# Transposing q and k in quarters, four at a time, in a fused attention and token-mixing kernel

## The chip, the cores and the metric

The kernel runs on one core of one Trainium2 chip. The metric is device time in microseconds for one execution of the whole program, the median over runs.

## The reference

For each of 4 batches and 8 heads of 64 channels, attention over 768 tokens in which a query sees the 96 tokens up to itself and the first 8 tokens; then a mixing block on the result.

```python
scores = (q @ k.T) / sqrt(D) - slope[h] * dist          # kept: local window of 96, and 8 global keys
a = softmax(where(keep, scores, -1e9));  x = a @ v      # x as [B, 768, 512]
theta = x @ w_theta
y = w_tok_r @ (x * cos(theta)) + w_tok_i @ (x * sin(theta))
u = x + y;  out = u + relu(u @ w_ch)
```

## The kernel before

Work is cut in tiles of 128 tokens, six to a batch, and heads go in pairs: the two heads of a pair fill the 128 partitions with their 64 channels each. A query tile needs the keys of its own tile and of one more tile (the previous one, whose first 8 columns are replaced by the global keys), so the scores of a pair are 11 blocks of 128x128 in three groups (`GROUPS`): group 0 holds tiles 0 and 1, groups 1 and 2 two tiles each.

Every instruction is put on its engine in the order in which the program is written (`K` keeps program order), so the order below is set by hand. For each pair of heads:

- `att_transpose` brings q and k of the pair from token-major to channel-major. It issues 12 TensorE transposes for q and 12 for k (six token tiles, two heads), each with a 128x64 block of q or k as the stationary operand and a 128x128 identity as the moving one, into two PSUM tiles `ps_tr` of one bank each, one for q and one for k. Then ScalarE copies k and VectorE or ScalarE (`q_eng`) copies q to SBUF (`kT`, `qT`). The copy interleaves: token number 6p+t of a head lies at partition p, place t, so the copies read with a stride.
- `att_extras`, on GpSimd, makes the key tiles in which the first 8 columns are the global keys (`kT[:, S:]`, lines 233 and 234), and `prepare_v` does the same for v (lines 91 and 92). The loads of the next batch (`load_heads`) stand behind them in GpSimd's queue.
- `att_scores` computes one group's scores in a two-bank PSUM tile `ps_w` (two buffers); the two heads of the pair use the two row halves of the array. ScalarE exponentiates it (line 279), VectorE multiplies by the mask and bias factors (`att_mul`, lines 290 and 292).
- `att_values` multiplies by v, with 65 columns of which the last sums the weights, and VectorE normalises.

Batch 0's attention runs first by itself with a different path for the bias. The attention of batches 1 to 3 runs inside `attend_beside`, between the token mixing (`mix_tok`, line 403, 128x512 matmuls) of the batch before. For each pair the order is: scores of group 0, four or eight mixing matmuls, scores of groups 1 and 2, the transposes of the next pair, eight mixing matmuls (`m(2)`), the values of this pair. The transposes for the first pair of a batch stand outside this loop: for batch 1 among the set-up of the token weights, for batches 2 and 3 between the theta matmuls of the batch before (`mix_theta`, line 368), whose sines ScalarE computes with another table (lines 376 and 377). `turn_u` sends u through a DMA transpose on SyncE's queue, and `mix_ch` (line 445) waits for it.

Of the kernel before, what the change touches and what calls it, by code (L numbers as in the profile page):

```python
# [10 lines left out]
BF = mybir.dt.bfloat16  # L11
# [5 lines left out]
def kernel(  # L17
# [13 lines left out]
    nc = tc.nc  # L31
    B, H, S, D = q.shape
    T = 128
    NT = S // T
    DM = H * D
    NC = DM // T
    NG = int(n_global)
# [11 lines left out]
    abuf = ctx.enter_context(tc.tile_pool(name="abuf", bufs=3))  # L49
# [4 lines left out]
    K = tc.keep_in_program_order  # L54

    def ps_wide():
        return psum.tile([T, 2, DM], FP, name="ps_w", tag="ps_w", bufs=2)
# [4 lines left out]
    def ps_tr(cols):  # L62
        return psum.tile([T, cols], BF, name="ps_tr", tag="ps_tr", bufs=2)
# [4 lines left out]
    q_sb, k_sb, x_sb = {}, {}, {}  # L68
# [19 lines left out]
    def prepare_v(b, h0, eng=nc.gpsimd):  # L88
        hs = slice(h0, h0 + 2)
        vs, vp = v_sb[b % 2], v_pv[b % 2]  # L90
        K(eng.tensor_copy(out=vp[:, hs, :, :], in_=vs[:, hs, 1:NT - 1, :]))
        K(eng.tensor_copy(
            out=vp[0:NG, hs, :, :],
            in_=vs[0:NG, hs, 0:1, :].to_broadcast([NG, 2, NT - 2, D + 1])))
# [56 lines left out]
    ident = const.tile([T, T], BF)  # L151
# [50 lines left out]
    for g_, blocks in enumerate(GROUPS):  # L202
        for i_, key in enumerate(blocks):
            where[key] = (g_, i_)
    qTs, kTs, exps, probs, values = {}, {}, {}, {}, {}
    xTs, zris, css = {}, {}, {}

    def att_transpose(b, h0, extras=True, sins=None, q_eng="dve", between=None, cuts=(T,)):
        pq, pk = ps_tr(S), ps_tr(S)
        for src, pst in ((q_sb[b], pq), (k_sb[b], pk)):  # L210
            if pst is pk and between is not None:
                between()
            for t_ in range(NT):
                for hh in range(2):
                    K(nc.tensor.transpose(pst[hh * D:(hh + 1) * D, t_ * T:(t_ + 1) * T],  # L215
                                          src[:, h0 + hh, t_ * D:(t_ + 1) * D], ident))
        if sins is not None:
            sins()

        kT = abuf.tile([T, S + (NT - 2) * T], BF, name="kT", bufs=2)  # L220
        qT = abuf.tile([T, S], BF, name="qT", bufs=2)
        copy = nc.scalar.copy if q_eng == "act" else nc.vector.tensor_copy
        for op, dst, src in ((nc.scalar.copy, kT[:, 0:S], pk), (copy, qT, pq)):
            for p0, p1 in zip((0,) + cuts, cuts):
                K(op(out=dst.rearrange("a (p t) -> a p t", t=NT)[:, p0:p1, :],  # L225
                     in_=src.rearrange("a (t p) -> a p t", t=NT)[:, p0:p1, :]))
        qTs[b, h0], kTs[b, h0] = qT, kT
        if extras:
            att_extras(b, h0)

    def att_extras(b, h0, eng=nc.gpsimd, values=True):
        kT = kTs[b, h0]
        K(eng.tensor_copy(out=kT[:, S:], in_=kT[:, T:S - T]))  # L233
        K(eng.tensor_copy(
            out=kT[:, S:].rearrange("a (t p) -> a t p", p=T)[:, :, 0:NG],
            in_=kT[:, None, 0:NG].to_broadcast([T, NT - 2, NG])))
        if eng is nc.gpsimd and values:
            prepare_v(b, h0)
# [3 lines left out]
    def att_bias(h0, g_):  # L242

        ps = biased[h0, g_] = ps_wide()
        rows = dist.rearrange("a n t -> a (n t)")
        for hh in range(2):
            if g_ == 0:
                out_, rhs = ps[:, hh, 0:3 * T], rows
            else:
                out_ = ps[:, hh, :].rearrange("a (r x) -> a r x", r=2)  # L250
                rhs = rows[:, None, T:3 * T].to_broadcast([T, 2, 2 * T])
            K(nc.tensor.matmul(out_, lhsT=ident_d[:, h0 + hh, :], rhs=rhs,
                               start=True, stop=False))

    def att_scores(b, h0, g_, mul=True):
        qT, kT = qTs[b, h0], kTs[b, h0]
        blocks = GROUPS[g_]
        n = len(blocks)
        bias = b == 0 and g_ != 1
        if bias and (h0, g_) not in biased:  # L260
            att_bias(h0, g_)
        ps = biased[h0, g_] if bias else ps_wide()

        runs = [(0, 2)] + [(2, 1)] if g_ == 0 else [(i_, 1) for i_ in range(n)]
        for i_, w in runs:
            it, prev = blocks[i_]
            kc = it * T if prev == 0 else (0 if it == 1 else S + (it - 2) * T)
            for hh in range(2):
                R = slice(D * hh, D * (hh + 1))
                K(nc.tensor.matmul(ps[:, hh, i_ * T:(i_ + w) * T],  # L270
                                   lhsT=kT[R, kc:kc + T], rhs=qT[R, it * T:(it + w) * T],
                                   start=not bias, stop=not bias or i_ == n - 1))
        if bias:
            p = abuf.tile([T, 2, 4 * T], BF, name="p", bufs=6)
            K(nc.scalar.activation(p[:, :, 0:n * T], ps[:, :, 0:n * T], AF.Exp, scale=scale))
            probs[b, h0, g_] = p
            return
        e = abuf.tile([T, 2, 4 * T], BF, name="e", bufs=3)
        K(nc.scalar.activation(e[:, :, 0:n * T], ps[:, :, 0:n * T], AF.Exp, scale=scale))  # L279
        exps[b, h0, g_] = e  # L280
        if mul:
            att_mul(b, h0, g_)

    def att_mul(b, h0, g_):
        e = exps[b, h0, g_]
        n = len(GROUPS[g_])
        p = abuf.tile([T, 2, 4 * T], BF, name="p", bufs=6)
        hs = slice(h0, h0 + 2)
        if g_ == 0:
            K(nc.vector.tensor_mul(p[:, :, 0:n * T], e[:, :, 0:n * T], wmask[:, hs, :]))  # L290
        else:
            K(nc.vector.tensor_mul(  # L292
                p.rearrange("a h (r x) -> a h r x", r=2),
                e.rearrange("a h (r x) -> a h r x", r=2),
                wmask[:, hs, None, T:3 * T].to_broadcast([T, 2, 2, 2 * T])))
        probs[b, h0, g_] = p
# [179 lines left out]
    def attend_beside(b, main, lead, load):  # L476


        def m(n=1):
            for _ in range(n):  # L480
                main.pop(0)()

        m(lead)
        for h0 in range(0, H, 2):
            att_scores(b, h0, 0)
            m(2 if h0 else 1)
            att_scores(b, h0, 1)
            att_scores(b, h0, 2)
            if h0 + 2 < H:
                att_transpose(b, h0 + 2, q_eng="act")  # L490
                if load and h0 == 0:
                    load_heads(b + 1, 0, 4)
                if load and h0 + 4 == H:
                    load_heads(b + 1, 4, 4)
                m(2)
            else:
                if load:
                    turn_x(b, NC - 2, False)
                m(len(main) - 1)
            att_values(b, h0)  # L500
            if h0 + 2 < H and not (load and h0 + 4 == H):
                turn_x(b, h0 // 2, True)
        m()
# [4 lines left out]
    for src, dst in ((first[:, 0], q_sb[0]), (first[:, 1], k_sb[0])):  # L508
        K(nc.vector.tensor_copy(out=dst[:, 0:2, :], in_=src))
    att_bias(0, 0)  # L510
    att_transpose(0, 0, extras=False, between=lambda: keep_warm(1), cuts=(43, T))
    make_ident_d(2, 6)
    att_extras(0, 0, nc.vector)
    prepare_v(0, 0, nc.vector)
    keep_warm(1)
    att_scores(0, 0, 0)
    att_scores(0, 0, 1)
    att_transpose(0, 2, extras=False)
    att_extras(0, 2, nc.gpsimd, False)
    prepare_v(0, 2)  # L520
    load_wtok(0)
# [118 lines left out]
```

## Time and profile before

| | |
|---|---|
| median of 3 runs | 174.29 us (173.44 to 175.55) |
| profiled execution | 173.54 us, span 171.8 us |
| granted TensorE clock | 1.0 |
| busy: PE / weight load / VectorE / ScalarE / GpSimd | 94% / 51% / 67% / 60% / 35% of the span |
| transposes of q and k (line 215) | 384 matmuls, 16.5 us busy |
| copies of them out of PSUM (line 225), ScalarE and VectorE | 12.9 + 7.5 us and 6.8 us busy |

Matmuls are pipelined, so the busy time of one (219 ns for a transpose) is its latency, not what it costs in a row of others; the distance between starts gives that. A wait is put down to what released the engine.

### The profile page before, as it was taken

Reading aid. Unit: us, or ns where it says so; the run is one execution under the profiler, and the core shown is the slowest. Engines: PE = TensorE matmul, PEld = TensorE weight load, DVE = VectorE, ACT = ScalarE, POOL = GpSimd, SP = SyncE. Lnnn points to the kernel's source line nnn. Section 1 sums busy time; section 2 is a strip of 40 time slices with the busy share of each in tenths; the row PEclk is TensorE's granted clock in tenths of the full one; section 3 lists DMA queues with packets and bytes.
Section 4 is the critical chain, followed back from the end, with each engine's and each line's share of the span. In section 5 each row is a group of like instructions: output and inputs, shape, how many; then the busy total and the mean of one; then the engine's idle time right before and its main releaser. Section 6 shows DMA issues by size and latency. Waiting matters only on the chain.

```text
span 171.8 us, 4076 instructions
## 1 busy us (share of the span) xinstructions
PE 162.1 (94%) x1700; PEld 87.5 (51%) x1700; DVE 114.2 (67%) x210; ACT 103.0 (60%) x120; POOL 60.9 (35%) x99
## 2 busy tenths in 40 slices
PE   7669999999999999999999998999999999999992
PEld 2246665556465654536556553545655544444441
DVE  7878865965858774767587694748567766634362
ACT  5969887947676562798658604798756708400010
POOL 8996797004672820033944700044134000000000
PEclk9999999999999999999999999999999999999999
DMA  5999999999999999910699999911433642233325
GB/s 151 188 170 189 209 211 209 196 183 179 173 142 148 114 229 199 250 64 4 81 167 118 152 210 197 213 65 22 89 77 94 84 152 86 96 34 61 103 109 185
DMA packets 57058, 24.05 MB, mean 140 GB/s; under 512 B 43088, under 2 KB 54096, under 8 KB 57040
## 3 DMA queue, kind: packets, MB, share of 16 engines
q0 software_dynamic: 35328, 12.45, 69.2%
q1 hardware_dynamic: 21440, 10.95, 29.6%
q10 hardware_dynamic: 272, 0.39, 0.7%
q8 instruction: 13, 0.21, 0.6%
q14 instruction: 5, 0.04, 0.1%
HBM read 25.69 MB, written 6.29 MB: 186 GB/s over the span
## 4 chain that ended last, share of the span: by engine, by line
PE 76%; DMA 9%; DVE 6%; POOL 3%; ACT 2%; issue 2%; DVEq 0%; POOLq 0%; ACTq 0%
PE ps_mm L403 34%; PE ps_mm L445 11%; PE ps_w L368 10%; PE ps_w L270 6%; PE ps_tr L215 6%; DMA uTd<-u 5%; PE ps_w L319 4%; DMA v_sb<-in_v_dram 4%; DVE w_tokT L117 2%; PE ps_mm L319 2%; PE ps_tr L114 1%; DVE zri L384 1%; ACT e L279 1%; DVE p L292 1%; ACT kT L225 1%
## 5 line engine op out<-in xcount | busy, mean ns | idle before, releaser
L403 PE MATMUL ps_mm<-zri,w_tokT 128*128 128x512 bf16 x288 | 68.7, 380 | 0.1
L279 ACT ACTIVATE e<-ps_w 128x1024 bf16<-128x1024 f32 (+1 forms) x40 | 37.1, 958 | 18.4 <-PE ps_w L270 18.4
L403 PEld LDWEIGHTS <-w_tokT 128*128 128x128 bf16 x288 | 26.2, 98 | 30.7 <-issue 2.3
L233 POOL COPY kT<-kT 128x512 bf16<-128x512 bf16 x15 | 9.6, 643 | 68.8 <-ACT kT L225 68.7
L292 DVE TENSOR_TENSOR p<-e,wmask 128x1024 bf16<-128x1024 bf16 x28 | 19.9, 709 | 12.2 <-ACT e L279 12.2
L376 ACT ACTIVATE cs<-ps_w,halfpi 128x1024 bf16<-128x1024 f32 x12 | 13.4, 1116 | 19.9 <-PE ps_w L368 19.8
L408 DVE TENSOR_TENSOR u<-x_sb,ps_mm 128x512 bf16<-128x512 bf16 x24 | 16.2, 683 | 12.5 <-PE ps_mm L403 12.5
L368 PE MATMUL ps_w<-w_theta_bf,xT 128*128 128x512 bf16 x96 | 22.8, 379 | 0.3 <-ACT cs L377 0.3
L445 PE MATMUL ps_mm<-w_ch_bf,uTd 128*128 128x512 bf16 x88 | 22.5, 379 | 0.5 <-DMA uTd<-u 0.5
L384 DVE TENSOR_TENSOR zri<-cs,x_sb 128x1024 bf16<-128x1024 bf16 x24 | 16.1, 690 | 9.7 <-ACT cs L376 8.4
L270 PE MATMUL ps_w<-qT,kT 64*128 64x128 bf16 (+1 forms) x320 | 16.0, 223 | 2.8 <-DVE qT L225 1.3
L448 DVE SCALAR_TENSOR_TENSOR o_sb<-ps_mm,u 128x512 f32<-128x512 f32 (+2 forms) x25 | 16.5, 665 | 1.1 <-PE ps_mm L445 0.9
L270 PEld LDWEIGHTS <-kT 64*128 64x128 bf16 x320 | 9.3, 94 | 12.8 <-issue 8.5
L225 ACT COPY kT<-ps_tr 128x768 bf16<-128x768 bf16 (+2 forms) x17 | 12.9, 765 | 2.9 <-PE ps_tr L215 2.8
L319 PEld LDWEIGHTS <-p 128*128 128x128 bf16 x352 | 12.7, 97 | 3.7 <-DVE p L292 0.5
L368 PEld LDWEIGHTS <-xT 128*128 128x128 bf16 x96 | 8.9, 98 | 10.9 <-issue 0.5
L445 PEld LDWEIGHTS <-uTd 128*128 128x128 bf16 x88 | 8.1, 97 | 9.9 <-DMA uTd<-u 1.2
L80 POOL DMA_DIRECT2D v_sb<-in_v_dram x10 | 13.1, 1309 | 0.0
L377 ACT ACTIVATE cs<-ps_w 128x1024 bf16<-128x1024 f32 x12 | 12.2, 1020 | 0.0
L327 DVE TENSOR_TENSOR x_sb<-ps_w,rec 128x768 bf16<-128x768 f32 x12 | 11.5, 958 | 0.4
L319 PE MATMUL ps_w<-v_sb,p 128*128 128x65 bf16 x168 | 10.3, 193 | 0.0
L430 ACT COPY uT<-ps_tr 128x512 bf16<-128x512 bf16 x1 | 0.6, 586 | 15.5 <-PE ps_tr L426 15.5
(79 smaller groups left out, 189.5 us busy)
## 6 DMA issues: line engine op xcount, KB each, us to landing
out_dram<-o_sb SPq DMA_DIRECT2D x23, 256.0 KB, 3.0
q_sb<-in_q_dram POOLq DMA_DIRECT2D x6, 384.0 KB, 7.7
k_sb<-in_k_dram POOLq DMA_DIRECT2D x6, 384.0 KB, 10.4
v_sb<-in_v_dram POOLq DMA_DIRECT2D x6, 384.0 KB, 15.1
w_nat<-in_moe_w_tok_r_dram POOLq DMA_DIRECT2D x1, 1152.0 KB, 12.5
w_nat<-in_moe_w_tok_i_dram POOLq DMA_DIRECT2D x1, 1152.0 KB, 13.6
v_sb<-in_v_dram POOLq DMA_DIRECT2D x4, 192.0 KB, 7.2
q_sb<-in_q_dram POOLq DMA_DIRECT2D x3, 192.0 KB, 6.7
```

The costliest lines, as they stand in the source:

```text
L225: K(op(out=dst.rearrange("a (p t) -> a p t", t=NT)[:, p0:p1, :], in_=src.rearrange("a (t p) -> a p t", t=NT)[:, p0:p1, :]))
L270: K(nc.tensor.matmul(ps[:, hh, i_ * T:(i_ + w) * T], lhsT=kT[R, kc:kc + T], rhs=qT[R, it * T:(it + w) * T], start=not bias, stop=not bias ...
L279: K(nc.scalar.activation(e[:, :, 0:n * T], ps[:, :, 0:n * T], AF.Exp, scale=scale))
L292: K(nc.vector.tensor_mul(p.rearrange("a h (r x) -> a h r x", r=2), e.rearrange("a h (r x) -> a h r x", r=2), wmask[:, hs, None, T:3 * T].t ...
L319: K(nc.tensor.matmul(dst, lhsT=lhsT, rhs=rhs, start=(i_ == 0), stop=(i_ == len(mms) - 1)))
L368: K(nc.tensor.matmul(pth[:, s2, :], lhsT=xTs[b][:, dc, c:c + T], rhs=w_theta_bf[:, dc, :], start=(dc == 0), stop=(dc == NC - 1)))
L376: K(nc.scalar.activation(cs[:, :, 0, :], pth, AF.Sin, bias=halfpi))
L384: K(nc.vector.tensor_mul(zris[b][:, st:st + 2, wi, :].rearrange("a s (c d) -> a s c d", d=T), cs[:, :, wi, :].rearrange("a s (c d) -> a s ...
L403: K(nc.tensor.matmul(acc, lhsT=w_tokT[wi][:, st, tt * T:(tt + 1) * T], rhs=zris[b][:, st, wi, :], start=(done[b, tt] == 0), stop=(done[b, ...
L408: K(nc.vector.tensor_add(us[b][:, tt, :].rearrange("a (c d) -> a c d", d=T), x_sb[b][:, :, tt, :], acc.rearrange("a (c d) -> a c d", d=T)))
L445: K(nc.tensor.matmul(pc[:, 0:N], lhsT=uT[:, c:c + T], rhs=w_ch_bf[:, dc, cols], start=(dc == 0), stop=(dc == NC - 1)))
L448: K(nc.vector.scalar_tensor_tensor(o_sb, in0=pc[:, 0:N], scalar=0.0, in1=us[b][:, tt, cols], op0=ALU.max, op1=ALU.add))
```

## The change

For batches 1 to 3, a 128x64 block is no longer transposed whole. Its 128 tokens are halved, so that each transpose takes 64 tokens by 64 channels: the row half of the array follows the token half `r`, the column half follows the head `hh`. Four such quarters, two heads by two token halves, follow one another in the queue, first of k and then of q for each tile. The two row halves write to two different PSUM banks, so a bank now holds q and k of one token half (`halves[r]`), where it held all tokens of q or of k. There are still two copies to SBUF: ScalarE takes the first bank, and the engine that copied q takes the second; each writes its half of q and of k into one combined tile `qk`. The copy of keys with the global columns, `mT`, is now a part of that tile. Batch 0 keeps whole transposes, but uses the combined tile.

```diff
     def att_transpose(b, h0, extras=True, sins=None, q_eng="dve", between=None, cuts=(T,)):
+        qk = abuf.tile([T, 2 * S + (NT - 2) * T], BF, name="qk", bufs=2)
+        kT, qT = qk[:, 0:S], qk[:, S:2 * S]
+        qTs[b, h0], kTs[b, h0] = qT, kT
+        mTs[b, h0] = qk[:, 2 * S:]
+        copy = nc.scalar.copy if q_eng == "act" else nc.vector.tensor_copy
+        if b > 0:
+            HP = T // 2
+            halves = [ps_tr(S), ps_tr(S)]
+            for t_ in range(NT):
+                for i_, src in enumerate((k_sb[b], q_sb[b])):
+                    c = (i_ * NT + t_) * HP
+                    for r in range(2):
+                        P = slice(r * HP, (r + 1) * HP)
+                        for hh in range(2):
+                            K(nc.tensor.transpose(
+                                halves[r][hh * D:(hh + 1) * D, c:c + HP],
+                                src[P, h0 + hh, t_ * D:(t_ + 1) * D], ident[P, P]))
+            if sins is not None:
+                sins()
+            for r, op in enumerate((nc.scalar.copy, copy)):
+                K(op(out=qk[:, 0:2 * S].rearrange("a (i r p t) -> a i r p t",
+                                                  i=2, r=2, t=NT)[:, :, r, :, :],
+                     in_=halves[r].rearrange("a (i t p) -> a i p t", i=2, t=NT)))
+            if extras:
+                att_extras(b, h0)
+            return
         pq, pk = ps_tr(S), ps_tr(S)
...
-        kT = abuf.tile([T, S + (NT - 2) * T], BF, name="kT", bufs=2)
-        qT = abuf.tile([T, S], BF, name="qT", bufs=2)
...
     def att_extras(b, h0, eng=nc.gpsimd, values=True):
-        K(eng.tensor_copy(out=kT[:, S:], in_=kT[:, T:S - T]))
+        K(eng.tensor_copy(out=mT, in_=kT[:, T:S - T]))
...
     def att_scores(b, h0, g_, mul=True):
-            kc = it * T if prev == 0 else (0 if it == 1 else S + (it - 2) * T)
+            if prev == 0 or it == 1:
+                keys = kT[:, (it - prev) * T:(it - prev + 1) * T]
+            else:
+                keys = mT[:, (it - 2) * T:(it - 1) * T]
```

More of the change, by code (lines that the diff above doesn't have):

```diff
@@ L204 @@
             where[key] = (g_, i_)
-    qTs, kTs, exps, probs, values = {}, {}, {}, {}, {}
+    qTs, kTs, mTs = {}, {}, {}
+    exps, probs, values = {}, {}, {}
     xTs, zris, css = {}, {}, {}
     def att_transpose(b, h0, extras=True, sins=None, q_eng="dve", between=None, cuts=(T,)):
+        qk = abuf.tile([T, 2 * S + (NT - 2) * T], BF, name="qk", bufs=2)
[24 more added lines that the diff above has]
+            return
         pq, pk = ps_tr(S), ps_tr(S)
@@ L216, in att_transpose @@
                                           src[:, h0 + hh, t_ * D:(t_ + 1) * D], ident))
-        if sins is not None:
-            sins()
-        kT = abuf.tile([T, S + (NT - 2) * T], BF, name="kT", bufs=2)
-        qT = abuf.tile([T, S], BF, name="qT", bufs=2)
-        copy = nc.scalar.copy if q_eng == "act" else nc.vector.tensor_copy
-        for op, dst, src in ((nc.scalar.copy, kT[:, 0:S], pk), (copy, qT, pq)):
+        for op, dst, src in ((nc.scalar.copy, kT, pk), (copy, qT, pq)):
             for p0, p1 in zip((0,) + cuts, cuts):
@@ L226, in att_transpose @@
                      in_=src.rearrange("a (t p) -> a p t", t=NT)[:, p0:p1, :]))
-        qTs[b, h0], kTs[b, h0] = qT, kT
         if extras:
@@ L232, in att_extras @@
         kT = kTs[b, h0]
-        K(eng.tensor_copy(out=kT[:, S:], in_=kT[:, T:S - T]))
+        mT = mTs[b, h0]
+        K(eng.tensor_copy(out=mT, in_=kT[:, T:S - T]))
         K(eng.tensor_copy(
-            out=kT[:, S:].rearrange("a (t p) -> a t p", p=T)[:, :, 0:NG],
+            out=mT.rearrange("a (t p) -> a t p", p=T)[:, :, 0:NG],
             in_=kT[:, None, 0:NG].to_broadcast([T, NT - 2, NG])))
@@ L255, in att_scores @@
     def att_scores(b, h0, g_, mul=True):
-        qT, kT = qTs[b, h0], kTs[b, h0]
+        qT, kT, mT = qTs[b, h0], kTs[b, h0], mTs[b, h0]
         blocks = GROUPS[g_]
@@ L270, in att_scores @@
                 K(nc.tensor.matmul(ps[:, hh, i_ * T:(i_ + w) * T],
-                                   lhsT=kT[R, kc:kc + T], rhs=qT[R, it * T:(it + w) * T],
+                                   lhsT=keys[R, :], rhs=qT[R, it * T:(it + w) * T],
                                    start=not bias, stop=not bias or i_ == n - 1))
```

## Prediction

> **What bounds the kernel now.** I read the page first (busy shares and the chain that ended last), then the groups by shape, then the timeline of one repetition of the changed step.
>
> ```profile
> span 171.8 us, 4076 instructions
> PE 162.1 (94%) x1700; PEld 87.5 (51%) x1700; DVE 114.2 (67%) x210; ACT 103.0 (60%) x120; POOL 60.9 (35%) x99
> ...
> PE 76%; DMA 9%; DVE 6%; POOL 3%; ACT 2%; issue 2%; DVEq 0%; POOLq 0%; ACTq 0%
> ```
>
> PE is busy 94% of the span and holds 76% of the chain. Read alone, that says that a microsecond taken from the transposes is a microsecond gained. The stage says otherwise. Here is one head pair of a later batch (batch 1, the transposes of pair 4) from the timeline; columns are start, length, engine, line, tiles and count:
>
> ```profile
> 47.22 0.62 PE L270 MATMUL ps_w<-qT,kT 64*128 64x128 bf16 x16
> 47.66 1.94 ACT L279 ACTIVATE e<-ps_w 128x1024 bf16<-128x1024 f32 x2 [1.36 <-PE ps_w L270]
> 47.77 0.53 PE L215 MATMUL ps_tr<-ident,q_sb 128*64 128x128 bf16 x12
> 48.13 0.50 PE L215 MATMUL ps_tr<-ident,k_sb 128*64 128x128 bf16 x12
> 48.56 1.90 PE L403 MATMUL ps_mm<-zri,w_tokT 128*128 128x512 bf16 x8
> 49.48 0.81 ACT L225 COPY kT<-ps_tr 128x768 bf16<-128x768 bf16 x1
> 50.16 0.83 ACT L225 COPY qT<-ps_tr 128x768 bf16<-128x768 bf16 x1
> 50.35 0.61 POOL L233 COPY kT<-kT 128x512 bf16<-128x512 bf16 x1 [0.96 <-ACT kT L225]
> ...
> 50.94 0.19 PE L319 MATMUL ps_w<-v_sb,p 128*128 128x65 bf16 x1
> ...
> 51.07 0.34 PE L270 MATMUL ps_w<-qT,kT 64*128 64x256 bf16 x4
> ```
>
> Two chains run from the scores of groups 1 and 2 (47.22) to the scores of the next pair's group 0 (51.07). PE does scores, 24 transposes, eight long matmuls and 22 value matmuls without a gap. ScalarE does two exponentials, then the k copy and the q copy, also without a gap, and ends at 50.16+0.83 = 50.99. The next scores need that q copy.
>
> How long after the copy can PE start? In the first pair of the batch PE did stand still for it:
>
> ```profile
> 44.23 0.83 ACT L225 COPY qT<-ps_tr 128x768 bf16<-128x768 bf16 x1
> 44.89 0.19 PE L319 MATMUL ps_w<-v_sb,p 128*128 128x65 bf16 x1
> 45.11 0.34 PE L270 MATMUL ps_w<-qT,kT 64*128 64x256 bf16 x4
> ```
>
> There 45.11 is 0.22 after the last value matmul's start, against 0.13 in the pair above, and 0.05 after the copy's end (45.06). So in the pair above ScalarE would have released PE at 50.99+0.05 = 51.04, and PE arrived at 51.07: only 0.03 us of PE's time can be saved there. Six of the nine pairs look like this; the last of the six is batch 3's:
>
> ```profile
> 129.79 0.83 ACT L225 COPY qT<-ps_tr 128x768 bf16<-128x768 bf16 x1
> 130.70 0.34 PE L270 MATMUL ps_w<-qT,kT 64*128 64x256 bf16 x4
> ```
>
> (130.70 against 129.79+0.83+0.05 = 130.67.) Batch 2's first pair, and batch 3's like it, has more room: 81.35 against 81.24, so 0.11.
>
> ```profile
> 80.36 0.83 ACT L225 COPY qT<-ps_tr 128x768 bf16<-128x768 bf16 x1
> 81.35 0.34 PE L270 MATMUL ps_w<-qT,kT 64*128 64x256 bf16 x4
> ```
>
> **The change part by part.** *Transposes.* The step runs 12 times (three later batches, four pairs each). Each time 24 matmuls of 128 rows by 64 columns with 128 moving columns become 48 of 64 by 64 with 64 moving columns, four to a set, twelve sets. What does a step cost today, and how many go at once?
>
> ```profile
> 41.84 0.36 PE L215 MATMUL ps_tr<-ident,q_sb 128*64 128x128 bf16 x6
> 59.68 0.51 PE L351 MATMUL ps_tr<-ident,x_sb 128*128 128x128 bf16 x6
> 47.62 0.22 PE L270 MATMUL ps_w<-qT,kT 64*128 64x128 bf16 x2
> 47.84 0.79 PE ps_tr L215 x24
> 50.47 0.67 PE ps_w L319 x22
> ...
> L270 PE MATMUL ps_w<-qT,kT 64*128 64x128 bf16 x288 | 14.1, 217 | 1.4 <-DVE kT L234 1.0 <-POOL kT L234 0.4
> L215 PE MATMUL ps_tr<-ident,k_sb 128*64 128x128 bf16 x192 | 8.1, 219 | 0.0
> ```
>
> (Three rows of the timeline, two of the chain of waits, two of the groups with busy time and mean ns.) The first row shows six of them in 0.36 us; the x12 row above has 0.53. Six more cost 0.17 us, or 0.057 per two. The full-array transposes of L351 have (0.51-0.219)/5 = 0.058 each (0.219 is about what one transpose lasts). So two half-array transposes go in the time of one: the array's column halves work side by side. The score matmuls show the same for the row halves: two of them last 0.22 us together, as long as one alone (217 ns). Nothing in this trace uses both cuts at once. The time per step with 64 moving columns is bounded by the value matmuls, 65 columns wide and back to back: 0.67/22 = 0.030 us. If four quarters go together, a set costs 0.030 and the step 12 x 0.030 = 0.36 where 12 x 0.057 = 0.68 stood: 0.32 us less, each time. If only two go together it is 24 x 0.030 = 0.72: 0.04 us more. I take 0.32, because both cuts are seen to overlap, each by itself. Weight loads double from 24 to 48, with 64 columns each as before; they run under the matmuls now and I cost them at nothing. Cover gone, they are the slower rival below. The change of array shape before and after the step stays, one each.
>
> *Where 0.32 is worth something.* In the nine steps inside the attention loop the saving goes first to the slack above: 6 x 0.03 + 2 x 0.11 + 0 (the pair that waited already) = 0.40 us. What is late next there is ScalarE's q copy, now the second copy: PE will stand about 0.25 us at L297's first score matmul of each pair, with the next token-mixing matmuls queued behind it. In the three steps that open a batch no such chain lies beside PE:
>
> ```profile
> 36.89 0.79 PE ps_tr L215 x24
> ...
> 70.17 0.79 PE ps_tr L215 x24
> 70.96 1.83 PE ps_w L368 x8
> ...
> 107.61 0.79 PE ps_tr L215 x24
> ```
>
> They stand on the chain that ended last. Behind the one at 70.17 come theta matmuls, whose sines ScalarE takes up late, then the copy, a table load and the first exponential:
>
> ```profile
> 71.22 1.02 ACT L377 ACTIVATE cs<-ps_w 128x1024 bf16<-128x1024 f32 x1
> 72.83 1.12 ACT L376 ACTIVATE cs<-ps_w,halfpi 128x1024 bf16<-128x1024 f32 x1 [0.60 <-PE ps_w L368]
> ```
>
> ScalarE was idle 0.60 before 72.83, so this chain moves earlier with PE by the whole 0.32. Three times 0.32 is 0.96.
>
> *Copies.* Still two per step, 128x768 each, on the same engines; each now holds one half of the tokens of q and of k. In the built program the first score matmul still waits for both copies, although its tokens lie in the first, so nothing is released earlier.
>
> ```profile
> L225 ACT COPY kT<-ps_tr 128x768 bf16<-128x768 bf16 x15 | 12.0, 803 | 2.9 <-PE ps_tr L215 2.8
> L225 ACT COPY qT<-ps_tr 128x768 bf16<-128x768 bf16 x9 | 7.5, 829 | 0.0
> L356 ACT COPY xT<-ps_tr 128x768 bf16<-128x768 bf16 x1 | 0.8, 799 | 0.2 <-PE ps_tr L351 0.2
> ```
>
> ScalarE's time hardly depends on the pattern: the plain copy of L356 takes 799 ns, the interleaving ones 803 and 829. I take no change; the ends are 18 copies x -0.03 and x +0.03, or 0.5 us either way.
>
> *GpSimd.* Its copy of the middle keys (L233, now L257) waited for the k copy and will wait for both: 50.99 in place of 50.29, 0.7 us later, and with it the key fix-up, the two value copies, and in every second pair the next batch's loads. The keys are needed by the score matmuls of groups 1 and 2, which start 2.1 us after group 0's (45.11 and 47.22): with 0.61 for the copy and a short fix-up they stay covered. The loads move past one tight place on DMA:
>
> ```profile
> 96.18 8.62 DMA uTd<-u
> ...
> 104.84 1.04 PE L445 MATMUL ps_mm<-w_ch_bf,uTd 128*128 128x512 bf16 x4 [0.51 <-DMA uTd<-u]
> ```
>
> (The first row is the chain's, the second the timeline's.) This transpose of u shares the DMA engines with the loads, and PE waits for it at 104.84. Loads issued 0.7 later may let it through sooner or keep it longer: -0.5 (that wait gone) to +0.7 (as late as the loads). I take 0, since the u that it moves is no later.
>
> **The sum.** 0.96 + 0.40 = 1.36 us. The profiled execution took 173.54 us (span 171.8 and 1.7 around it), so it becomes 172.2. The median of the three runs is 174.29, 0.75 above that execution; on it the same 1.36 gives 172.9, which is my forecast. Its own range is 172.0 to 174.0, by the copies and the DMA. A measurement of this kernel can tell about 1% (1.7 us) from no change, so I expect a gain that barely shows.
>
> **The rivals.** *The saving counts in full.* If ScalarE's chain gives way, 12 x 0.32 = 3.8 us: 170.5. For it stands only that PE is 76% of the chain; against it the 0.03 us in six pairs. Chance 0.11.
>
> *Four at a time doesn't happen.* Quarters go in twos, 0.72 against 0.68: 12 x 0.04 = 0.5 us more, 174.8, or with a little overlap no change. For it: no row shows both cuts at once. Chance 0.19.
>
> *PE's queue can't supply them (slower).* Each step issues 96 instructions in place of 48. The fastest sustained pace in the trace is one load and one matmul per 0.0285 us (0.057/2), and 0.030 in the value matmuls. If that were the supply, 48 would take 1.37 us. The queue holds some ahead:
>
> ```profile
> L270 PEldq EVENT_SEMAPHORE  x1: 51/51/51, 50.4 to 50.4; - x1
> ```
>
> PE's sequencer has come to the score matmuls of 51.07 at 50.4, some 17 value matmuls ahead. So 31 of the 48 come at 0.0285: 0.88 against 0.68, 0.20 more, in eleven of twelve steps (the waiting pair hides half of one): 2.3 us, 176.6. It decides from 0.68/31 = 0.022 us per matmul with its load; below that there is a gain. Against it: the sequencer is that far ahead right after the fast transposes, so it isn't at its limit at 0.0285. Chance 0.19.
>
> (The Trainium skill, "TensorE: Matmul & The Clock Gate", section "Wait — 56ns, not 53.3ns?", speaks for this rival: matmuls start no closer than about 25 ns however few columns they move. Taken for the whole array, an estimate by it is 48 x 0.025 = 1.2 us a step, and a time near 180. Taken for each part of the array by itself it costs nothing here; the first reading is 0.04 of this rival's 0.19. The two scores that last 0.22 us together started closer than that, so the trace takes the second reading for a short burst; no run here shows it for 48.)
>
> *Copies or loads late (slower).* Each copy 0.1 longer, as a new pattern might cost, and PE kept 0.7 longer for u: 18 x 0.1 + 0.7 - 1.36 = +1.1, 175.4; with twice that on the copies it passes 1%. Against it: 799 beside 803 and 829 ns. Chance 0.06.
>
> **How the numbers follow.** Forecast 0.45 (a third of it beyond 1%), full gain 0.11, no overlap 0.19, supply 0.19, late copies or loads 0.06. Faster by over 1%: 0.16 of the forecast and 0.11 of the full gain, 0.27. Slower by over 1%: 0.19 of the supply, 0.03 of the late copies and 0.02 of no overlap, 0.24. The rest, 0.49, is within 1%. The range takes in the forecast, no overlap, late copies and the supply case to its value; outside stay the full gain and a supply slower still, less than 2 in 10: 171.0 to 176.6.
>
> **What would show it.** Right: the transposes' 24 in 0.79 us become 48 in about 0.45, with the first and twelfth quarter starting some 0.06 apart; matmuls of 64 columns last about 0.19; ScalarE's copies stay at 0.80 to 0.83; PE idles 0.2 to 0.3 before the first score matmul in seven to nine pairs, ended by ScalarE's copy; the distance from scores to scores in the loop stays within 0.05. Wrong: quarters 0.014 us apart or more on average (no overlap or supply; supply shows as a fast start and a slow rest), copies over 0.9, a longer wait for uTd near 104, or a loop that shortens by 0.3 per pair.

## The result, and the profile after

The changed kernel takes 171.32 us (median of 6 runs, 171.30 to 171.63), the kernel before 173.34 in the same comparison (6 runs, 173.06 to 175.55): a ratio of 0.988, 95% interval 0.985 to 0.990. A second comparison on another chip, among the experiments below, gave 0.992 (0.988 to 0.995). The change gains about 1%. A few executions, in some of the runs below, are slow ones; the ratios are of the others, the medians of all.

The profiled execution took 171.33 us. The page's span, its row of engines and its chain that ended last:

```profile
span 169.5 us, 4624 instructions
...
PE 158.7 (94%) x1965; PEld 86.2 (51%) x1988; DVE 114.7 (68%) x210; ACT 103.0 (61%) x120; POOL 63.2 (37%) x99
...
PE 80%; DVE 6%; DMA 4%; issue 3%; POOL 3%; ACT 3%; DVEq 0%; ACTq 0%; POOLq 0%
```

PE's share of the chain rose from 76% to 80% although it does less; DMA's fell from 9% to 4%. That is the first sign that not all of the gain is TensorE's.

The timeline of the pair that the prediction showed (start, length, engine, line, tiles, count):

```profile
47.12 0.22 PE L226 MATMUL ps_tr<-ident,k_sb 64*64 64x64 bf16 x4
47.17 0.20 PE L226 MATMUL ps_tr<-ident,q_sb 64*64 64x64 bf16 x4
...
47.49 0.21 PE L226 MATMUL ps_tr<-ident,q_sb 64*64 64x64 bf16 x4
...
48.83 1.51 ACT L232 COPY qk<-ps_tr 128x768 bf16<-128x768 bf16 x2
48.98 0.69 DVE L319 TENSOR_TENSOR p<-e,wmask 128x1024 bf16<-128x1024 bf16 x1 [0.22 <-ACT e L306]
...
49.55 0.19 PE L346 MATMUL ps_w<-v_sb,p 128*128 128x65 bf16 x1
49.73 0.20 PE L346 MATMUL ps_w<-v_pv,p 128*128 128x65 bf16 x1
...
50.16 0.19 PE L346 MATMUL ps_w<-v_sb,p 128*128 128x65 bf16 x1
50.39 0.34 PE L297 MATMUL ps_w<-qk 64*128 64x256 bf16 x4
```

Twelve sets of four start between 47.12 and 47.49. The ten gaps after 47.17 take 0.32 us, 0.032 for a set of four, where before a pair of halves took 0.057: all four quarters of the array work at once. But PE then stands still twice: the value matmuls, 0.03 apart otherwise, jump from 49.55 to 49.73, some 0.15 us, as VectorE's product p ends at 48.98+0.69 = 49.67; and the next scores start 0.23 after the last value matmul, where 0.13 is the pace, because ScalarE's second copy ends at 48.83+1.51 = 50.34.

The chain of waits has the transposes as whole steps (start, length, instructions); the first, third and fourth rows are the steps that open a batch:

```profile
36.52 0.51 PE ps_tr L226 x48
47.19 0.51 PE ps_tr L226 x48
...
69.47 0.51 PE ps_tr L226 x48
...
105.80 0.51 PE ps_tr L226 x48
```

Each is 0.28 shorter than before's 0.79 for 24. What that brings in the loop is read from group 0's scores. Batch 2's first and last of four, in the timeline of before and then of after:

```profile
76.18 0.34 PE L270 MATMUL ps_w<-qT,kT 64*128 64x256 bf16 x4
93.25 0.34 PE L270 MATMUL ps_w<-qT,kT 64*128 64x256 bf16 x4
```

```profile
75.20 0.34 PE L297 MATMUL ps_w<-qk 64*128 64x256 bf16 x4
92.12 0.34 PE L297 MATMUL ps_w<-qk 64*128 64x256 bf16 x4
```

Three steps save 17.07-16.92 = 0.15 us there (0.11, 0.02 and 0.02), where the transposes alone save 0.84. Batches 1 and 3, read in the same way, give 0.05 and 0.16.

The last difference is the wait for u. Before, and after:

```profile
101.59 1.02 PE L445 MATMUL ps_mm<-w_ch_bf,uTd 128*128 128x512 bf16 x4
```

```profile
100.46 1.02 PE L472 MATMUL ps_mm<-w_ch_bf,uTd 128*128 128x512 bf16 x3
103.05 1.03 PE L472 MATMUL ps_mm<-w_ch_bf,uTd 128*128 128x512 bf16 x4
```

From one channel mixing to the next it was 3.25 us (to 104.84, which waited for DMA); it is 2.59, with no wait: 0.66 less. What such a distance has above its length without a wait is called time lost at u below.

So the span's 2.3 us fall apart into 0.37 ahead of the first changed step (36.89 to 36.52), 3 x 0.28 = 0.84 in the opening steps, 0.05+0.15+0.16 = 0.36 in the loop, and 0.66 at the wait for u; together 2.23. Only 1.20 of it is time that the transposes saved directly. The first part has none of the later batches' transposes in it.

### The profile page after: what moved, and what is told of

Same layout as the page of the kernel before. It is cut to its first block, busy times and chain, and to the rows that moved or that the text cites. A ratio compares the mean times of both kernels' runs of the same rounds, so it can differ in the third digit from the quotient of the medians.

```text
span 169.5 us, 4624 instructions
## 1 busy us (share of the span) xinstructions
PE 158.7 (94%) x1965; PEld 86.2 (51%) x1988; DVE 114.7 (68%) x210; ACT 103.0 (61%) x120; POOL 63.2 (37%) x99
## 4 chain that ended last, share of the span: by engine, by line
PE 80%; DVE 6%; DMA 4%; issue 3%; POOL 3%; ACT 3%; DVEq 0%; ACTq 0%; POOLq 0%
PE ps_mm L430 35%; PE ps_mm L472 12%; PE ps_w L395 11%; PE ps_w L297 7%; PE ps_w L346 5%; DMA v_sb<-in_v_dram 4%; PE ps_tr L226 3%; PE ps_mm L346 2%; ACT e L306 2%; PE ps_tr L114 2%; DVE zri L411 1%; DVE w_tokT L117 1%; PE ps_tr L378 1%; DVE p L319 1%; ACT qk L249 1%
## 5 line engine op out<-in xcount | busy, mean ns | idle before, releaser
L430 PE MATMUL ps_mm<-zri,w_tokT 128*128 128x512 bf16 x276 | 67.0, 380 | 1.3 <-issue 0.8
L257 POOL COPY qk<-qk 128x512 bf16<-128x512 bf16 x15 | 9.5, 636 | 65.2 <-ACT qk L232 53.0
L472 PE MATMUL ps_mm<-w_ch_bf,uTd 128*128 128x512 bf16 x82 | 21.5, 379 | 0.6 <-issue 0.5
L297 PE MATMUL ps_w<-qk 64*128 64x128 bf16 (+1 forms) x320 | 16.1, 223 | 2.3 <-DVE qk L249 0.8
L232 ACT COPY qk<-ps_tr 128x768 bf16<-128x768 bf16 x21 | 16.0, 815 | 2.0 <-issue 2.0
L297 PEld LDWEIGHTS <-qk 64*128 64x128 bf16 x320 | 10.0, 94 | 12.1 <-issue 7.8
L346 PEld LDWEIGHTS <-p 128*128 128x128 bf16 x352 | 13.2, 97 | 4.6 <-DVE p L319 0.8
L92 POOL COPY v_pv<-v_sb 8x520 bf16<-8x520 bf16 x15 | 11.5, 767 | 0.9
L346 PE MATMUL ps_w<-v_sb,p 128*128 128x65 bf16 x168 | 11.3, 193 | 0.0
```

The lines of the kernel that those rows point to most:

```text
L232: K(op(out=qk[:, 0:2 * S].rearrange("a (i r p t) -> a i r p t", i=2, r=2, t=NT)[:, :, r, :, :], in_=halves[r].rearrange("a (i t p) -> a i ...
L297: K(nc.tensor.matmul(ps[:, hh, i_ * T:(i_ + w) * T], lhsT=keys[R, :], rhs=qT[R, it * T:(it + w) * T], start=not bias, stop=not bias or i_ ...
L346: K(nc.tensor.matmul(dst, lhsT=lhsT, rhs=rhs, start=(i_ == 0), stop=(i_ == len(mms) - 1)))
L430: K(nc.tensor.matmul(acc, lhsT=w_tokT[wi][:, st, tt * T:(tt + 1) * T], rhs=zris[b][:, st, wi, :], start=(done[b, tt] == 0), stop=(done[b, ...
L472: K(nc.tensor.matmul(pc[:, 0:N], lhsT=uT[:, c:c + T], rhs=w_ch_bf[:, dc, cols], start=(dc == 0), stop=(dc == NC - 1)))
```

## The experiments

The theory tested: four quarters go at once; in the loop ScalarE's second copy takes most of it back; and the loads, which GpSimd now issues later, let the transposing DMA of u through sooner. The rivals: the two parts of the gain are otherwise divided, or the wait for u and the start vary by themselves.

### The kernel before, once more

> The kernel before, unchanged, profiled once more. If the first 0.37 us (up to the first transposes of batch 1) and the 0.67 us wait for u near 104 us belong to the kernel, both are there again within 0.05. If they are chance of DMA and of the port that VectorE and GpSimd share, one or both differ by 0.2 us or more.

Measured: 172.86 us. The start of batch 1's opening step in the chain, for this execution, and for one of the changed kernel taken later:

```profile
36.25 0.79 PE ps_tr L215 x24
```

```profile
36.95 0.51 PE ps_tr L226 x48
```

All profiles taken have this step between 36.25 and 36.95, the kernel before at both 36.25 and 36.89, the changed one at 36.52 and 36.95. So the 0.37 us of the start-up are within what one kernel varies by, and can't be laid on the change. The wait for u moved too: 0.49 longer near 67 us, 0.56 shorter near 104. Over both places the kernel before loses 0.66 in one profile and 0.59 in the other.

### Quarters in the opening steps alone

```diff
-        if b > 0:
+        if b > 0 and h0 == 0:
```

> Quarters only in the three steps that open a batch, whole transposes elsewhere. Theory (only these steps pay in full, ScalarE's copies cap the loop): 0.28 us each, 0.85 us of the 1.21 that the steps brought, and the loop's pairs stay as before. Rival (every step pays alike): 3 of 12 parts, 0.30 us.

(The path of whole transposes also calls `sins`, as the kernel before does; the same holds for the next run.) Measured: 174.01 us, ratio 1.0005 (0.9966 to 1.0043). The three steps take 0.51 in place of 0.79, as in the changed kernel, but the time didn't fall. PE's waits for u, in a table of waits from 60 to 110 us (total, times, longest), in before and then here:

```profile
PEld L445 <- DMA uTd<-u: 1.2, 2, 1.0
PE ps_mm L445 <- DMA uTd<-u: 0.5, 1, 0.5
```

```profile
PEld L474 <- DMA uTd<-u: 2.0, 2, 1.2
PE ps_mm L474 <- DMA uTd<-u: 1.0, 2, 0.7
```

The expectations add the two rows of such a table, here 3.0 for 1.7; but the load and its matmul wait over the same stretch, so the sum counts time twice. By the distances between channel mixings 1.36 us are lost at u here, 0.66 in before. PE comes to u sooner and waits longer for it: the transpose of u that it waits for near 104 us lands 68.0 us after batch 1's opening step here, and 67.9 in both profiles of the kernel before. The loads start as before here, since in the loop the old order of copies is kept.

### Quarters in the loop alone

```diff
-        if b > 0:
+        if b > 0 and h0 > 0:
```

> Quarters only in the nine steps inside the attention loop. Theory: 0.02 to 0.03 us in six pairs, 0.11 in two, nothing in the one that waited already, 0.36 us in all, with PE idle 0.2 us or more ahead of the next pair's scores. Rival (every step pays alike): 0.9 us or more. GpSimd's later loads are in this kernel and not in x_open: if they end the wait for u near 104 us, it is gone here, and another 0.67 us with it.

Measured: 172.33 us, ratio 0.9947 (0.9919 to 0.9976). The loop's steps save 0.36 in the trace, as in the changed kernel. The wait for u is gone from the table. Of the 0.9 us of gain the transposes account for less than half.

### The same quarters, two at a time

```diff
-            for t_ in range(NT):
-                for i_, src in enumerate((k_sb[b], q_sb[b])):
-                    c = (i_ * NT + t_) * HP
-                    for r in range(2):
+            for r in range(2):
+                for t_ in range(NT):
+                    for i_, src in enumerate((k_sb[b], q_sb[b])):
+                        c = (i_ * NT + t_) * HP
```

> The same 48 quarters, but all of the first token half and then all of the second, so that two neighbours in the queue share the row half and at most two go at once. Theory (the row and the column cut overlap together): a step goes back to about 0.72 us + 0.1, so that the three opening steps lose their 0.28 each, 0.85 us slower than the changed kernel or more. Rival (the gain is in the shorter moving side alone): a step stays at 0.51 us.

Measured: 173.12 us, ratio 0.998 (0.9955 to 1.001). The step in the chain (one record is missing):

```profile
36.52 0.78 PE ps_tr L226 x47
```

With one row half after the other, 48 quarters take what 24 halves took. The gain of the step is the overlap of the row halves, not the shorter moving side. (Each row half writes to its own PSUM bank, in every run; none tells the two apart.)

### q copied before k, with the old transposes

```diff
-        for op, dst, src in ((nc.scalar.copy, kT[:, 0:S], pk), (copy, qT, pq)):
+        pair = ((nc.scalar.copy, kT[:, 0:S], pk), (copy, qT, pq))
+        for op, dst, src in pair[::-1] if q_eng == "act" else pair:
```

> The kernel before, but where ScalarE makes both copies it copies q first and k second, so that GpSimd's copy of the keys and the loads that it issues behind it start some 0.7 us later, as they do in the changed kernel, with the transposes as they were. Theory (the wait for the channel-major u before the channel mixing near 67 and 104 us went away because GpSimd's loads start later and no longer share the DMA queues with the transposing DMAs): the waits of TensorE for u fall from 1.7 us in the window from 60 to 110 to under 0.3, and the time falls by 0.3 to 0.7 us: 172.7 to 173.0, ratio 0.996 to 0.998. Rival (these waits vary from execution to execution and the change has no part in them): waits between 0.9 and 2 us, ratio 1.000 within 0.002.

Measured: 172.43 us, ratio 0.9944 (0.9927 to 0.9961): somewhat more than half a per cent, and more than was expected, with no change on TensorE. Near 95 us the timelines show what moved: loads on GpSimd, the transposing DMA on SyncE. Before, and then this kernel:

```profile
94.59 0.76 POOL L75 DMA_DIRECT2D q_sb<-in_q_dram  x1
95.34 0.76 POOL L75 DMA_DIRECT2D k_sb<-in_k_dram  x1
96.07 1.46 POOL L80 DMA_DIRECT2D v_sb<-in_v_dram  x1
96.18 1.21 SPq L417 DMA_TRANSPOSE uTd<-u  x1
```

```profile
94.91 0.76 POOL L75 DMA_DIRECT2D q_sb<-in_q_dram  x1
95.57 1.20 SPq L418 DMA_TRANSPOSE uTd<-u  x1
95.65 0.76 POOL L75 DMA_DIRECT2D k_sb<-in_k_dram  x1
```

The changed kernel:

```profile
94.41 0.76 POOL L75 DMA_DIRECT2D q_sb<-in_q_dram  x1
95.05 1.20 SPq L444 DMA_TRANSPOSE uTd<-u  x1
95.16 0.75 POOL L75 DMA_DIRECT2D k_sb<-in_k_dram  x1
```

Before, u's transpose is issued behind three loads; here, and in the changed kernel, behind one. The wait for u is gone, and the loop's steps are as long as before to 0.02.

### The changed kernel with early loads

```diff
+        if b > 0 and h0 > 0:
+            prepare_v(b, h0)
         K(eng.tensor_copy(out=mT, in_=kT[:, T:S - T]))
...
-        if eng is nc.gpsimd and values:
+        if eng is nc.gpsimd and values and not (b > 0 and h0 > 0):
             prepare_v(b, h0)
```

> The changed kernel, but in the steps within the loop GpSimd makes the two copies of the shifted values ahead of the copy of the keys, in the 3.6 us in which it would wait for ScalarE; the loads that it issues behind start about 1.4 us earlier than in the changed kernel, 1.1 us earlier against the transposing DMAs than in the kernel before. Theory (part of what the change gained is that later loads let the transposing DMA of u get ahead of them): TensorE's waits for u between 60 and 110 us come back to 1.5 to 3 us in place of none, and the time is 0.5 to 1.2 us above the changed kernel's: 171.8 to 172.6, ratio to the kernel before 0.991 to 0.996. Rival (the waits come and go by themselves): no waits or one, 171.2 to 171.6, ratio 0.987 to 0.990.

Measured: 173.62 us, ratio 0.9993 (0.9973 to 1.0014), worse than either side expected: the whole gain is gone, with the transposes at 0.51 as before it. The loop's steps, added up for each batch, are as long as the changed kernel's within 0.04; what is new is the wait. The two rows add to 4.6; the time lost at u is 2.10 us, about the change's whole gain of 2.0:

```profile
PEld L474 <- DMA uTd<-u: 2.8, 2, 1.9
PE ps_mm L474 <- DMA uTd<-u: 1.8, 2, 1.4
```

The time from issue to landing of u's transposes between 55 and 112 us, in before, the changed kernel, the one with q copied first, and this one:

```profile
DMA to landing us min/median/max: 2.4/7.8/9.1
```

```profile
DMA to landing us min/median/max: 2.4/6.5/8.5
```

```profile
DMA to landing us min/median/max: 2.4/6.5/8.1
```

```profile
DMA to landing us min/median/max: 2.4/8.5/9.6
```

In these four, the earlier the loads, the longer the median. (The Trainium skill, "DMA: Bandwidth & Descriptors", section "Queues, rings and completion order", says that each DMA engine takes turns between the queues that have work for it, a packet at a time. By that, a load that is issued ahead of the transpose slows it from the start; these four medians agree, but one run below doesn't: with the values in another order the median is 8.0, though u is issued behind one load as in the changed kernel.)

### The changed kernel, once more

> The changed kernel itself once more, for how much TensorE's wait for u varies from one execution to another. Theory (with the later loads the wait is mostly gone, not always): waits for u between 60 and 110 us of 0 to 0.9 us, 171.2 to 171.7 us, ratio 0.987 to 0.991. Rival (the profile of the changed kernel without any wait was a lucky one): over 1.5 us of waits and 171.8 to 172.6, ratio 0.991 to 0.995.

Measured: 171.86 us, ratio 0.9915 (0.9883 to 0.9947), just past the theory's time and into the rival's; but the waits for u are 0.5 us in its profile, as the theory has it, and that execution was late from the start (the 36.95 above, 0.43 after the first profile). So neither is settled for the time. Eight profiles in all have u behind one load at both places. In seven of them, up to 110 us, 0 to 0.34 us are lost at u; the eighth, with the values in another order, loses 1.22, though near 95 us its loads and u are issued within 0.02 of the changed kernel's times. With later loads the wait is mostly gone, not always, and the order of issue isn't all that sets it; what else does stays open.

### A tile in halves

```diff
-                K(op(out=qk[:, 0:2 * S].rearrange("a (i r p t) -> a i r p t",
-                                                  i=2, r=2, t=NT)[:, :, r, :, :],
+                K(op(out=qk[:, r * S:(r + 1) * S].rearrange("a (i p t) -> a i p t", i=2, t=NT),
```

(Readers of `qk` find their tokens in the new places.)

> The changed kernel with another order in the tile that receives the copies: k of half 0, q of half 0, k of half 1, q of half 1. Each copy then writes one unbroken stretch, and the scores of tiles 0 and 1 read the first stretch alone, so they need only the first of ScalarE's two copies. Theory (in the loop the 0.28 us that each step saves is given back because TensorE waits for ScalarE's second copy, some 0.8 us after the first, before the first scores): that wait goes, and the next one is for the products p in the value matmuls, some 0.16 us; each of the nine steps inside the loop gains about 0.1 us over the changed kernel, together 0.5 to 1.0: 170.3 to 170.8 us, ratio to the kernel before 0.983 to 0.986. Rival (ScalarE's own chain of two copies and three exponentials is full and sets the step whatever TensorE waits for): nothing is gained, 171.3, ratio 0.988, and the wait moves to the second group of scores or to the values.

Measured: 170.89 us, ratio 0.9859 (0.9822 to 0.9896). The first two of these pairs' scores in the timeline:

```profile
44.57 0.34 PE L307 MATMUL ps_w<-qk 64*128 64x256 bf16 x4
50.40 0.34 PE L307 MATMUL ps_w<-qk 64*128 64x256 bf16 x4
```

5.83 us for a step where before had 5.96 (45.11 to 51.07) and after 5.93: the 0.1 us that the theory gives. The time is just above the theory's range, and its interval overlaps the changed kernel's; in this profile 0.34 us are lost at u, near 108 us.

### The value matmuls in another order

```diff
-        for hh in range(2):
+        phs = [ps_acc() if apart else po[:, hh, :] for hh in range(2)]
+        tiles = range(NT)
+        for hh, its in ([(0, tiles), (1, tiles)] if apart else
+                        [(0, tiles[:4]), (1, tiles[:4]), (0, tiles[4:]), (1, tiles[4:])]):
...
-            for it in range(NT):
+            for it in its:
```

> The changed kernel with the new order of the value matmuls alone (tiles 0 to 3 of both heads, then 4 and 5), the receiving tile as in the changed kernel. Theory (two waits, one behind the other; the later one is for ScalarE's second copy): the wait for p in the value matmuls goes and the wait before the first scores grows by as much, 171.1 to 171.5 us, ratio 0.986 to 0.989. Rival (the wait for p is the one that sets the step and the reordered tile only counts for little): 169.2 to 170.0, ratio 0.976 to 0.981.

Measured: 171.85 us, ratio 0.99 (0.9847 to 0.9953). The loop's steps are the changed kernel's to 0.01 us; that the time is above the theory's lies at u, where this profile loses 1.22 us. In the loop the wait has only moved:

```profile
50.18 0.34 PE L297 MATMUL ps_w<-qk 64*128 64x256 bf16 x4 [0.19 <-ACT qk L232]
56.11 0.34 PE L297 MATMUL ps_w<-qk 64*128 64x256 bf16 x4 [0.20 <-ACT qk L232]
```

The wait for p is gone and PE stands before the scores instead, for ScalarE's second copy.

### Both: the tile in halves and the new order of the values

> As the run before it in this call (tile in halves), and the value matmuls of both heads take tiles 0 to 3 first and tiles 4 and 5 last, so that the products of the third score group are needed later. Theory (the give-back in the loop is two waits one behind the other, for the second copy and for p): with both out of the way each step inside the loop keeps up to its 0.28 us instead of 0.02 to 0.11; nine steps by 0.2 to 0.25 is about 2 us: 169.0 to 169.6 us, ratio to the kernel before 0.975 to 0.979. Rival (ScalarE's chain is full): 171.0 to 171.4, ratio 0.987, the same as the changed kernel.

The edit is the two above together. Measured: 169.01 us (169.00 to 169.02), ratio 0.9747 (0.9732 to 0.9761): the best kernel of this study.

```profile
44.32 0.34 PE L307 MATMUL ps_w<-qk 64*128 64x256 bf16 x4
49.99 0.34 PE L307 MATMUL ps_w<-qk 64*128 64x256 bf16 x4
```

5.67 us for a step: 0.29 less than before, so with both waits out of the way the loop keeps all that the transposes save. (In batch 1's first pair a wait for p is left.) ScalarE's chain isn't full: it waits 0.17 us for PE's scores before the exponential of group 0. No wait for u is in the table.

### The second copy on VectorE

```diff
-                att_transpose(b, h0 + 2, q_eng="act")
+                att_transpose(b, h0 + 2)
```

> The changed kernel with the second of the two copies in the loop on VectorE in place of ScalarE, so that both run at once. Theory (TensorE waits for the second copy because it starts when the first is done): the copies are done some 0.6 to 0.8 us earlier, the first scores no longer wait, the loads start earlier by as much; what is left is the wait for p, longer by what VectorE now does late (0.95 us more for each step on an engine that is 67 per cent busy): between 0.1 us less and 0.3 us more in each of nine steps, 170.5 to 174.0, ratio 0.983 to 1.003. Rival (the second copy's place doesn't matter): 171.3, ratio 0.988.

Measured: 175.04 us, ratio 1.0068 (1.0034 to 1.0102), slower than the theory's range. Its premise was wrong: the copies don't run at once.

```profile
49.13 0.69 DVE L319 TENSOR_TENSOR p<-e,wmask 128x1024 bf16<-128x1024 bf16 x1 [0.22 <-ACT e L306]
...
50.74 0.34 PE L297 MATMUL ps_w<-qk 64*128 64x256 bf16 x4 [0.23 <-DVE qk L232]
```

VectorE comes to its copy after the product that ends at 49.82, takes 952 ns for it, and the scores wait for that. Seven of the loop's nine steps are 0.20 to 0.21 longer than the changed kernel's, two are 0.50 longer, and 1.35 us are lost at u, which near 96 us is issued behind two loads.

### The quarters twice

```diff
-            for t_ in range(NT):
+            for t_ in [*range(NT), *range(NT)]:
```

> The changed kernel with the 48 quarters of each step issued twice, 96 in a row; one look for how long a run of them goes at its rate. Theory (four quarters of the array work at once and a set of four with its weight loads takes 0.032 us for as long as it is fed): the 96 take about 0.8 us in place of 0.4, and a step of the loop is longer by about 0.4 less what the waits absorb. Rival (the 48 go fast only because their instructions stand ready in the queue; beyond that the queue gives one instruction in some 22 ns, as the prediction's slower rival had it): the second 48 with their 48 loads take about 2 us, and each step grows by 2 us, the whole kernel by over 20 us. Between: at the 8 ns that lie between the loads late in a step the second 48 take 0.8 us.

Measured: 181.03 us, a single execution. The step in the chain:

```profile
36.49 0.91 PE ps_tr L226 x96
```

The second 48 with their 48 loads take 0.91-0.51 = 0.40 us, 0.008 for a matmul with its load, and the last are not slower than the first. The rival's 2 us don't come. But one of the twelve runs of 96, the second, is broken after 59 of them:

```profile
41.62 0.60 PE ps_tr L226 x59
42.22 1.10 issue
43.32 0.48 PE ps_tr L226 x37
```

The kernel as a whole lost 9.7 us, more than 12 x 0.40 = 4.8. PE's longest stops with nothing in the profile that ends them are this one of 1.1 us, one of 1.9 and one of 3.0 that ends at 97.12. What these stops are wasn't settled; a supply of instructions that runs short now and then isn't ruled out for this kernel. (The DMA queue that the profile names instruction has 20 packets here and 15 in the changed kernel, and one of them falls between 40 and 41.6, one between 57 and 59.9 and one between 94 and 95.5 us, about where the stops begin. That fits, but shows no cause.) In the changed kernel PE has no such stop above 0.2 us, and every step that the chain shows takes 0.51.

## Why the prediction was right or wrong

The forecast of 172.9 us was 1.6 too high. The result lies inside the widest range, 171.0 to 176.6, near its low end, but below the 172.0 to 174.0 that the forecast itself was given. None of its terms leads to 171.3, so that the wide range takes the result in is in part luck. By its own steps:

- *The cost of a step.* 0.36 in place of 0.68 was predicted. The sets come 0.032 apart, against 0.030 taken from the value matmuls, and the chain shows 0.51 for the 48, where about 0.45 was to show it right; so a step became 0.28 shorter, not 0.32. The reasoning from two overlaps, each seen by itself, to both together held; only the size was off.
- *The opening steps.* 0.96 predicted, 0.84 in the trace. That they count in full was right for the changed kernel only: alone, with the loads as before, they gained nothing, since PE then waited longer for u. The prediction had no term that ties them to the DMA.
- *The loop.* 0.40 predicted, 0.36 found, pair by pair as worked out: nothing in the waiting pair, 0.11 in two, 0.02 to 0.03 in six. The cause is the one named, ScalarE's second copy: without that wait (tile in halves) and without the one for p, the step keeps 0.29. The place was half right: PE stands some 0.15 for p inside the values and 0.10 before the scores. The prediction looked for 0.2 to 0.3 at the scores and didn't see that the products are the next to be late.
- *The copies.* No change was taken, and there is none: the group of ScalarE's copies after has a mean of 815 ns, against 803 and 829 before.

```profile
L232 ACT COPY qk<-ps_tr 128x768 bf16<-128x768 bf16 x21 | 16.0, 815 | 2.0 <-issue 2.0
```

- *The loads.* This is the step that failed. Later loads were taken as 0, between -0.5 and +0.7, "since the u that it moves is no later". The reason speaks of when u is ready, not of what is issued ahead of it. The wait of 104.84 went, 0.66 in this pair of profiles, outside the bound. The old kernel with the two copies swapped, whose TensorE work is the same, gained 0.56% (0.39 to 0.73), about 1.0 us; its trace loses nothing at u, which accounts for about 0.66 of that. The changed kernel with early loads lost everything. The order of issue was there to be read before: the first of the three loads at 94.59, u's transpose at 96.18. The 0.7 us of delay worked out for GpSimd would have put u ahead of the third load (96.07) and 0.14 short of the second (95.34). In the trace GpSimd's copy of the keys does start 0.73 later, counted from the next pair's first scores, but its last value copy (line 92) also takes 0.82 us where it took 0.61, as it does with the two copies swapped; with both, the loads come 0.95 later and u is ahead of two. Why that copy is longer isn't shown.
- *The base of the sum.* 172.2 on the profiled execution became 172.9 on a median of three runs, 174.29. Later comparisons have before at 173.34 to 173.61, so the profiled execution, 173.54, was the better base; that choice is 0.75 of the error. The remaining 0.85 is, in this pair of profiles, 0.66 at u and 0.37 at the start, less the 0.16 by which the transposes brought less than 1.36. The part at the start is luck, as the spread of 36.25 to 36.95 shows.

The rivals. *Four at a time doesn't happen*: false, as 0.51 and the run in twos (0.78) show. *PE's queue can't supply them*: false; the limit of 0.0285 for a load and a matmul, read off a pair of transposes, was the array's time and not the queue's, and 96 in a row keep 0.008 where the run isn't broken. (The prediction set the Trainium skill, "TensorE: Matmul & The Clock Gate", section "Wait — 56ns, not 53.3ns?", beside this rival, with its floor of about 25 ns between starts. For 48 and 96 quarters that floor doesn't hold across the whole array, and for each quarter by itself, at 32 ns, it isn't reached.) *The saving counts in full*: not in the changed kernel; with both waits removed it does, and the time is 169.01. *Copies or loads late*: the copies took as long as before; the loads came later, and it was a gain.

## What to carry to other kernels

When a saving makes one engine early, look for everything else that it will then meet: here a copy, a product and a DMA each took their part, and the first wait hid the second. Where a change moves the issue of a large load, write down which transfers on the other queues stand before and behind it; that order was worth 0.66 us here, beside 1.20 from the transposes. And take out waits that lie behind one another together: one of them alone gained 0 to 0.1 us a step, both 0.27.

## What the runs showed of the hardware that was not expected

Row halves and column halves of the array work side by side: four 64x64 transposes with their loads every 0.032 us, kept up for 96 in a row in all but one of twelve runs. With 24 more matmuls and 24 more loads a step than before, PE's queue was no limit. And start-up code with the same work ran 0.7 us longer or shorter from one execution to the next (36.25 to 36.95 us; 36.25 and 36.89 for the kernel before alone), over a third of the change's gain.
